# Load order of an mLSTM cell with a mixture-of-depths layer: broadcast maxima with each chunk, layer weights later, output gates half a batch ahead

## The chip, the cores and the metric

The kernel runs on one core of a Trainium2 chip. The metric is the device time of the program in microseconds, the median of several runs. The profile is one execution, recorded by the hardware profiler.

## What is computed

Two blocks stand behind each other. The first is an mLSTM cell over 4 batches of 8 heads, 768 steps, head dimension 40. It is written as a recurrence over steps, with a running maximum m that keeps the exponentials in range:

```python
m_new = np.maximum(f_gate[:, :, t] + m, i_gate[:, :, t])
f_stab = np.exp(f_gate[:, :, t] + m - m_new)
i_stab = np.exp(i_gate[:, :, t] - m_new)
C = f_stab * C + i_stab * np.einsum('bhd,bhe->bhde', vt, kt)
n = f_stab * n + i_stab * kt
h_tilde = np.einsum('bhde,bhe->bhd', C, qt)
denom = np.maximum(np.abs(np.einsum('bhd,bhd->bh', n, qt)), 1.0)
y[:, :, t] = sigmoid(o_gate[:, :, t]) * h_tilde / denom
```

The heads side by side give x (4, 768, 320). The second block scores each token (x times w_gate), takes the 128 best of each batch, puts them through relu(xe @ w1) @ w2 (320 to 1024 to 320), and writes x + sigmoid(score) times that; all other tokens pass through unchanged.

## The kernel before, in words

The 768 steps of a batch are cut into 6 chunks of 128, so that 24 chunks run one after the other, batch by batch, with a state C that goes from chunk to chunk. Ahead of them, a preamble on 32 partitions (batch times head) computes the running maxima of all chunks from the two gate inputs (L138 to L155). Each chunk's maxima `Mg` go to DRAM (`M_d`, L150), since every chunk later wants them broadcast over 128 partitions (`Mb`, L173).

One chunk (`mlstm_chunk`) is this. `Mb` is masked on GpSimd (POOL, affine_select, L174), and eight exponentials on ScalarE (ACT, L178) make the weights `W`. k and q are transposed on TensorE (PE, L185, `pt`) and copied out by ScalarE (`qkT`, L186). `pS` (L195) is the product of k and q, VectorE (DVE) multiplies it with `W` (`P`, L197), `pI` (L204) is what the state gives, `pC` (L218) the state's update, `pH` (L233) the result of the chunk. VectorE adds and scales (`num`, `den`, `rec`), GpSimd multiplies the gate in (`sor`, L245), VectorE writes `x` (L246) and the score `sc` (L249), and GpSimd issues two stores of the chunk, to `x_d` and to `out` (L252). The weights `W`, the maxima `Mb` and most other work tiles have 3 buffers.

After a batch's last chunk, `depths` ranks the tokens (`ge`, `pcol`, `rank`, `sel`), gathers the chosen rows (`xe`), transposes them (`pX`), runs both layers (`ph` L318, `py` L324, copied by ScalarE as `hT`, L320) and scatters `ye` into `out` (L327), behind which the stores of x to `out` wait. Its instructions stand between those of the next batch's first chunks. A scheduler at build time sets the order on each engine; each engine then works in that order.

Loads are issued on SyncE's queue (SPq): k, q and v of a chunk two chunks ahead into 4 rotating buffers (`qk`, `v`, L98, L99), the output gates `so` of a whole batch when it begins (L334, six loads, then one sigmoid over all, L335), and `Mb` of a chunk when the chunk itself is written. The layer weights (`w1`, `w2`, 2.5 MB) and `wg` are loaded by GpSimd's queue after the first batch's gates (L162 to L167). ScalarE needs another function table for the sigmoid than for the exponentials, so each change between them is an ACT_TABLE_LOAD.

Below, chunk 0 to chunk 5 are those of a batch, batch 0 to batch 3.

## Time and profile before

| what | value |
|---|---|
| median of 3 runs | 277.78 us (277.69 to 279.12) |
| profiled execution, its own time | 275.82 us |
| its span, first to last instruction | 274.1 us |
| PE busy | 196.6 us (72%) |
| DVE busy | 153.0 us (56%) |
| ACT busy | 115.8 us (42%) |
| POOL busy | 108.5 us (40%) |
| DMA | 41.08 MB in 107086 packets, mean 150 GB/s |

No engine is busy throughout, so the shares alone name no bound. A profile here is read by stages: what each stage waits for last. The profiled execution took 1.7 us more than its span, and 0.7% less than the median.

### The profile page before, as it was taken

What the parts mean: (1) busy time and instruction counts of PE and PEld (TensorE: products, weight loads), DVE (VectorE), ACT (ScalarE), POOL (GpSimd) and SP (SyncE); (2) the same over time, 40 slices, a digit from 0 to 9 for tenths busy, and PEclk for the clock granted to TensorE, in tenths of its full rate; (3) what the DMA queues carried; (4) which work ended last, traced back from release to release, by engine and by line L of the source; (5) the groups of instructions that cost most, each with busy time, mean ns of one, the idle gap of its engine ahead of it and who ended that gap; (6) DMA issues with size and microseconds to landing.
All of it is one profiled execution on the core that took longest, in us unless ns stands there. A gap on an engine that the chain in (4) does not pass through costs nothing.

```text
span 274.1 us, 6273 instructions
## 1 busy us (share of the span) xinstructions
PE 196.6 (72%) x2402; PEld 164.5 (60%) x2402; DVE 153.0 (56%) x443; ACT 115.8 (42%) x285; POOL 108.5 (40%) x155
## 2 busy tenths in 40 slices
PE   0463089987837999878798997777699998612980
PEld 0442068975626888766677976656488786501860
DVE  5800026597966407878768523897877088873100
ACT  2531486337287653636654181553543325100000
POOL 9900155167264203565454314545463055221001
PEclk9995555599995599999799999797869999965696
DMA  8799997599998633999999709597725041210000
GB/s 119 86 347 183 209 220 196 105 244 188 230 254 241 114 80 82 220 225 246 199 229 190 170 0 215 163 195 223 198 65 134 26 144 57 86 60 24 2 0 24
DMA packets 107086, 41.08 MB, mean 150 GB/s; under 512 B 101328, under 2 KB 101520, under 8 KB 107056
## 3 DMA queue, kind: packets, MB, share of 16 engines
q1 hardware_dynamic: 103680, 28.71, 54.3%
q0 software_dynamic: 3376, 11.96, 13.1%
q8 instruction: 19, 0.31, 0.6%
q14 instruction: 11, 0.09, 0.1%
HBM read 32.05 MB, written 8.62 MB: 148 GB/s over the span
## 4 chain that ended last, share of the span: by engine, by line
PE 31%; DVE 24%; issue 15%; DMA 12%; POOL 7%; SPq 6%; ACT 3%; POOLq 1%; DVEq 0%; ACTq 0%
PE ph L318 6%; PE pS L195 6%; DMA Mb<-M_d 6%; PE pH L233 5%; PE py L324 5%; DVE P L197 4%; DVE C L226 3%; POOL sor L245 3%; PE pI L204 3%; DVE ge L270 3%; SPq L98 2%; PE pt L185 2%; DVE x L246 2%; DVE C L228 2%; SPq L334 2%
## 5 line engine op out<-in xcount | busy, mean ns | idle before, releaser
L178 ACT ACTIVATE W<-Mb,cols 128x128 f32<-128x128 f32 x192 | 59.9, 391 | 34.5 <-POOL Mb L174 19.5
L233 PE MATMUL pH<-v,P 128*64 128x64 f32 x768 | 35.8, 249 | 19.0 <-DVE num L207 11.2
L186 ACT COPY qkT<-pt 128x512 f32<-128x512 f32 x48 | 26.9, 582 | 51.8 <-PE pt L185 51.3
L233 PEld LDWEIGHTS pH<-v,P 128*64 128x64 f32 x768 | 30.3, 157 | 26.7 <-DVE num L207 13.3
L185 PE MATMUL pt<-ident,qk 128*128 128x128 f32 x192 | 35.4, 318 | 15.1 <-ACT so L335 8.4
L195 PE MATMUL pS<-qkT 64*128 64x128 f32 x384 | 39.3, 324 | 1.7 <-ACT qkT L186 1.6
L174 POOL TENSOR_SCALAR_AFFINE_SELECT Mb<-Mb 128x1024 f32<-128x1024 f32 x24 | 26.7, 1116 | 31.3 <-DMA Mb<-M_d 31.3
L185 PEld LDWEIGHTS pt<-ident,qk 128*128 128x128 f32 x192 | 23.8, 158 | 19.6 <-ACT so L335 8.8
L195 PEld LDWEIGHTS pS<-qkT 64*128 64x128 f32 x384 | 31.4, 216 | 6.6 <-ACT qkT L186 3.2
L245 POOL TENSOR_TENSOR sor<-so,rec 128x320 f32<-128x320 f32 x24 | 17.4, 726 | 43.2 <-DVE rec L243 38.0
L197 DVE TENSOR_TENSOR P<-pS,W 128x512 f32<-128x512 f32 x48 | 31.9, 681 | 4.3 <-PE pS L195 3.6
L204 PE MATMUL pI<-C,qkT 128*64 128x128 f32 x320 | 25.9, 301 | 0.7 <-DVE C L228 0.7
L318 PE MATMUL ph<-xeT,w 128*128 128x128 f32 x192 | 25.3, 298 | 0.6 <-DVE g L303 0.6
L318 PEld LDWEIGHTS ph<-xeT,w 128*128 128x128 f32 x192 | 24.6, 212 | 1.6 <-DVE g L303 1.0
L246 DVE TENSOR_TENSOR x<-num,sor 128x320 f32<-128x320 f32 x20 | 12.1, 604 | 19.5 <-POOL sor L245 19.5
L212 POOL TENSOR_TENSOR wv<-v,cols 128x328 f32<-128x328 f32 x20 | 15.1, 755 | 19.1 <-PE pC L218 10.9
L204 PEld LDWEIGHTS pI<-C,qkT 128*64 128x64 f32 x320 | 19.9, 149 | 4.0 <-issue 1.1
L252 POOL DMA_DIRECT2D x_d<-x x24 | 14.0, 582 | 19.2 <-DVE x L246 18.6
L326 DVE SCALAR_TENSOR_TENSOR ye<-py,g,xe 128x320 f32<-128x320 f32 x4 | 2.2, 551 | 34.4 <-PE py L324 34.4
L270 DVE SCALAR_TENSOR_TENSOR ge<-sb,sc,earlier 128x512 bf16<-128x512 f32 (+5 forms) x24 | 16.9, 720 | 3.2 <-ACT sb L262 3.2
L226 DVE TENSOR_TENSOR C<-C,Mb 40x164 f32<-40x164 f32 x32 | 18.3, 571 | 0.5
L324 PE MATMUL py<-w,hT 128*128 128x320 f32 x64 | 17.9, 432 | 0.0
(83 smaller groups left out, 233.2 us busy)
## 6 DMA issues: line engine op xcount, KB each, us to landing
Mb<-M_d SPq DMA_DIRECT2D x24, 516.0 KB, 5.1
qk<-in_k_dram SPq DMA_DIRECT2D x24, 160.0 KB, 4.2
qk<-in_q_dram SPq DMA_DIRECT2D x24, 160.0 KB, 4.7
v<-in_v_dram SPq DMA_DIRECT2D x24, 160.0 KB, 4.2
so<-in_o_gate_dram SPq DMA_DIRECT2D x24, 160.0 KB, 4.2
x_d<-x POOLq DMA_DIRECT2D x24, 160.0 KB, 3.4
out_dram<-x POOLq DMA_DIRECT2D x24, 160.0 KB, 4.0
w<-in_moe_w_dram POOLq DMA_DIRECT2D x1, 1280.0 KB, 10.2
```

Of the source, the lines that this page charges most:

```text
L174: nc.gpsimd.affine_select(out=Mb[:, :, 0:L], in_=Mb[:, :, 0:L], compare_op=OP.is_ge, fill=BIG, base=0, pattern=[[0, H], [1, L]], channel_m ...
L178: nc.scalar.activation(out=W[:, h // 2, h % 2, :], in_=Mb[:, h, 0:L], func=AF.Exp, bias=cols[c][:, 0, b * H + h:b * H + h + 1], scale=-1.0)
L185: nc.tensor.transpose(pt[:, p, :], qk[:, j, 2 * p:2 * p + 2, :].rearrange("s a d -> s (a d)"), ident)
L186: nc.scalar.copy(out=qkT[:, j], in_=pt)
L195: nc.tensor.matmul(pS[j][:, p, :], qkT[e, 0, p, :], qkT[e, 1, p, :], start=True, stop=True)
L197: nc.vector.tensor_tensor(out=P[:, :, j, :], in0=pS[j], in1=W[:, :, j, :], op=OP.mult)
L204: nc.tensor.matmul(pI[t, 2 * p:2 * p + 2, :].rearrange("t a d -> t (a d)"), qkT[:, 1, p, t], C[:, p].rearrange("e a d -> e (a d)"), start= ...
L226: nc.vector.tensor_tensor(out=Cj, in0=Cj, op=OP.mult, in1=decay[e, :, j, L:L + 1].to_broadcast([D, NP, D1]))
L233: nc.tensor.matmul(pH[t, h, :], P[:, h // 2, h % 2, t], v1[:, h, :], start=True, stop=True)
L245: nc.gpsimd.tensor_tensor(out=sor, in0=so[:, c], in1=rec.unsqueeze(2).to_broadcast([128, H, D]), op=OP.mult)
L318: nc.tensor.matmul(ph[:, f, :], w1[:, j, (f0 + f) * 128:(f0 + f + 1) * 128], xeT[:, j, :], start=(j == 0), stop=(j == NDC - 1))
L324: nc.tensor.matmul(py, hT[:, f, :], w2[:, f, :], start=(f == 0), stop=(f == NFC - 1))
```

## The change

The load of `Mb` moves from the chunk itself into `load_chunk`, so that it is issued two chunks ahead, with 4 buffers in place of 3. The stores of `M_d` go from SyncE's queue to ScalarE's. The layer weights are issued when the second chunk is reached (`n == 1`), with `wg` alone left in front. The gates of batch 0 are loaded in two parts, chunks 0 and 1 with their k, q and v, the others after, with a sigmoid for each part. The gates of each later batch are loaded, and put through the sigmoid, in the middle of the batch before (`c == NT // 2`). The memsets of the k, q and v buffers write the padding alone.

```diff
--- before.py
+++ after.py
@@ -88,8 +88,8 @@
     qk_t = [const.tile([128, 2, H, DP], FP, name=f"qk{n}") for n in range(NB)]
     v_t = [const.tile([128, H, DP], FP, name=f"v{n}") for n in range(NB)]
     for n in range(NB):
-        nc.gpsimd.memset(qk_t[n], 0.0)
-        nc.gpsimd.memset(v_t[n], 1.0)
+        nc.gpsimd.memset(qk_t[n][:, :, :, D:DP], 0.0)
+        nc.gpsimd.memset(v_t[n][:, :, D:DP], 1.0)
 
     def load_chunk(b, c):
         n = (b * NT + c) % NB
@@ -97,7 +97,9 @@
         for j, src in enumerate((k, q)):
             nc.sync.dma_start(out=qk_t[n][:, j, :, 0:D], in_=src[b, :, t, :].rearrange("h p d -> p h d"))
         nc.sync.dma_start(out=v_t[n][:, :, 0:D], in_=v[b, :, t, :].rearrange("h p d -> p h d"))
-        return qk_t[n], v_t[n]
+        Mb = work.tile([128, H, L + 1], FP, name="Mb", bufs=NB)
+        nc.sync.dma_start(out=Mb, in_=_bcast(M_d[c][b * H:(b + 1) * H, :], 128))
+        return qk_t[n], v_t[n], Mb
 
     ident = const.tile([128, 128], FP, name="ident")
     make_identity(nc, ident)
@@ -147,7 +149,7 @@
         nc.scalar.activation(out=wk[:, c, :], in_=a[:, c, :], func=AF.Exp, bias=nM[:, c:c + 1], scale=1.0)
         nc.vector.tensor_copy(out=Mg[:, c, L:L + 1], in_=r[:, c, L - 1:L])
         M_d.append(dram.tile([BH, L + 1], FP, name=f"M_d{c}"))
-        nc.sync.dma_start(out=M_d[c], in_=Mg[:, c, :])
+        nc.scalar.dma_start(out=M_d[c], in_=Mg[:, c, :])
         pc = ps_t.tile([128, 3, BH], FP, name="pc", tag="t")
         for j, row in enumerate((a, wk, r)):
             nc.tensor.transpose(pc[:, j, :], row[:, c, :], ident[0:BH, 0:BH])
@@ -158,19 +160,18 @@
     w1 = const.tile([128, NDC, F_], FP, name="w1")
     w2 = const.tile([128, NFC, DM], FP, name="w2")
 
+    nc.gpsimd.dma_start(out=wg, in_=_bcast(moe_w_gate, 128))
+
     def load_weights():
-        nc.gpsimd.dma_start(out=wg, in_=_bcast(moe_w_gate, 128))
         if HW[-1][1] < 128:
             nc.gpsimd.memset(w1[:, NDC - 1, :], 0.0)
         for j, (d0, w) in enumerate(HW):
             nc.gpsimd.dma_start(out=w1[0:w, j, :], in_=moe_w1[d0:d0 + w, :])
         nc.gpsimd.dma_start(out=w2, in_=moe_w2.rearrange("(f p) d -> p f d", p=128))
 
-    def mlstm_chunk(b, c, qk, v1, C, so, x, sc):
+    def mlstm_chunk(b, c, qk, v1, Mb, C, so, x, sc):
         hs = slice(b * H, (b + 1) * H)
         k_n, q_n = qk[:, 0], qk[:, 1]
-        Mb = work.tile([128, H, L + 1], FP, name="Mb")
-        nc.sync.dma_start(out=Mb, in_=_bcast(M_d[c][hs, :], 128))
         nc.gpsimd.affine_select(out=Mb[:, :, 0:L], in_=Mb[:, :, 0:L], compare_op=OP.is_ge, fill=BIG, base=0,
                                 pattern=[[0, H], [1, L]], channel_multiplier=-1)
         W = work.tile([128, NP, 2, L], FP, name="W")
@@ -328,31 +329,47 @@
                                          out_offset=bass.IndirectOffsetOnAxis(ap=idx[:, 1:2], axis=0),
                                          in_=ye, in_offset=None, bounds_check=B * S - 1, oob_is_err=False)
 
+    def load_gates(b, so, c):
+        nc.sync.dma_start(out=so[:, c], in_=o_gate[b, :, c * L:(c + 1) * L, :].rearrange("h p d -> p h d"))
+
     def open_batch(b):
         so = ob.tile([128, NT, H, D], FP, name="so")
-        for c in range(NT):
-            nc.sync.dma_start(out=so[:, c], in_=o_gate[b, :, c * L:(c + 1) * L, :].rearrange("h p d -> p h d"))
-        nc.scalar.activation(out=so, in_=so, func=AF.Sigmoid)
         C = ob.tile([128, NP, 2, DP], FP, name="C")
         nc.gpsimd.memset(C, 0.0)
         x = xp.tile([128, NT, DM], FP, name="x")
         sc = xp.tile([128, NT], FP, name="sc")
         return C, so, x, sc
 
+    def sigmoid(so, c0, c1):
+        nc.scalar.activation(out=so[:, c0:c1], in_=so[:, c0:c1], func=AF.Sigmoid)
+
+
 
     steps = [(b, c) for b in range(B) for c in range(NT)]
-    loaded = {}
+    loaded, state = {}, {0: open_batch(0)}
+    EARLY = 2
     for n, (b, c) in enumerate(steps):
         for step in steps[n:n + AHEAD + 1]:
             if step not in loaded:
                 loaded[step] = load_chunk(*step)
-        if c == 0:
-            state = open_batch(b)
+                if step[0] == 0 and step[1] < EARLY:
+                    load_gates(0, state[0][1], step[1])
+                    if step[1] == EARLY - 1:
+                        sigmoid(state[0][1], 0, EARLY)
         if n == 0:
+            for g in range(EARLY, NT):
+                load_gates(0, state[0][1], g)
+            sigmoid(state[0][1], EARLY, NT)
+        if n == 1:
             load_weights()
-        mlstm_chunk(b, c, *loaded[b, c], *state)
+        if c == NT // 2 and b + 1 < B:
+            state[b + 1] = open_batch(b + 1)
+            for g in range(NT):
+                load_gates(b + 1, state[b + 1][1], g)
+            sigmoid(state[b + 1][1], 0, NT)
+        mlstm_chunk(b, c, *loaded[b, c], *state[b])
         if c == NT - 1:
-            depths(b, *state[2:])
+            depths(b, *state[b][2:])
 
 
 # ---- launch: one core; inputs and outputs as the reference has them ----
```

In the program as built, the start changes as follows. First SyncE's queue before, from the second chunk's k and q on (buffer numbers: qk_94 and v_98 are chunk 0, qk_95 chunk 1, qk_96 chunk 2, M_d_156 the maxima of chunk 0).

```order
L98 DMA qk_95<-in_q_dram 128x8x40
L150 DMA M_d_156<-Mg 32x129
...
L150 DMA M_d_236<-Mg 32x129
L99 DMA v_99<-in_v_dram 128x8x40
L98 DMA qk_96<-in_k_dram 128x8x40
L98 DMA qk_96<-in_q_dram 128x8x40
L99 DMA v_100<-in_v_dram 128x8x40
L334 DMA so<-in_o_gate_dram 128x8x40 x6
L173 DMA Mb<-M_d_156 128x1032
```

SyncE's queue in the changed kernel, from chunk 0's gate on:

```order
L333 DMA so<-in_o_gate_dram 128x8x40
L98 DMA qk_95<-in_k_dram 128x8x40
L98 DMA qk_95<-in_q_dram 128x8x40
L99 DMA v_99<-in_v_dram 128x8x40
L333 DMA so<-in_o_gate_dram 128x8x40
L101 DMA Mb<-M_d_156 128x1032
L101 DMA Mb<-M_d_172 128x1032
L98 DMA qk_96<-in_k_dram 128x8x40
L98 DMA qk_96<-in_q_dram 128x8x40
L99 DMA v_100<-in_v_dram 128x8x40
L101 DMA Mb<-M_d_188 128x1032
L333 DMA so<-in_o_gate_dram 128x8x40 x4
```

The maxima of chunk 0 now stand behind 8 loads in place of 15, and the last gate of batch 0 stands behind the maxima of three chunks. ScalarE in the changed kernel, in the same place (so 128x640 are two chunks' gates, 128x1280 the other four):

```order
L344 ACT_TABLE_LOAD
L344 ACTIVATE so<-so 128x640
L187 COPY qkT<-pt 128x512 x2
L179 ACT_TABLE_LOAD
L179 ACTIVATE W<-Mb,cols_162 128x128 x8
L187 COPY qkT<-pt 128x512 x2
L179 ACTIVATE W<-Mb,cols_178 128x128 x2
L344 ACT_TABLE_LOAD
L344 ACTIVATE so<-so 128x1280
L179 ACT_TABLE_LOAD
L179 ACTIVATE W<-Mb,cols_178 128x128 x6
```

Before, one sigmoid stood ahead of all exponentials; now the second one stands between the second and the third of chunk 1's eight. On the whole, ScalarE has 11 table loads in place of 9.

The second place is TensorE around the layers of batch 0 (pX, ph, py), between the first chunks of batch 1, which are pH with v_100 (chunk 0), v_101 (chunk 1) and v_98 (chunk 2). Before:

```order
L308 MATMUL pX<-ident,xe_130 128x128 x3
L233 MATMUL pH<-v_100,P 64x64 x7
L195 MATMUL pS<-qkT 128x128 x2
L318 MATMUL ph<-xeT,w_245 128x128 x24
L324 MATMUL py<-w_246,hT 128x320 x8
L195 MATMUL pS<-qkT 128x128 x6
L204 MATMUL pI<-C,qkT 64x128 x8
L218 MATMUL pC<-wv,qk_97 64x41 x8
L185 MATMUL pt<-ident,qk_94 128x128 x4
L233 MATMUL pH<-v_101,P 64x64 x16
```

The changed kernel:

```order
L219 MATMUL pC<-wv,qk_97 64x41 x8
L234 MATMUL pH<-v_101,P 64x64 x16
L196 MATMUL pS<-qkT 128x128
L309 MATMUL pX<-ident,xe_130 128x128 x3
L196 MATMUL pS<-qkT 128x128 x3
L205 MATMUL pI<-C,qkT 64x128 x3
L319 MATMUL ph<-xeT,w_245 128x128 x24
L325 MATMUL py<-w_246,hT 128x320 x8
L205 MATMUL pI<-C,qkT 64x128 x5
L219 MATMUL pC<-wv,qk_94 64x41 x8
L186 MATMUL pt<-ident,qk_95 128x128 x3
L234 MATMUL pH<-v_98,P 64x64 x16
```

Before, one chunk of batch 1 stood ahead of the layers; now two do, and the third is begun. At the two later batch ends, two chunks stand ahead of the layers in both kernels.

The third place is GpSimd behind the scatter of batch 1. Before:

```order
L327 DMA out_dram<-ye,idx 3072x320
L252 DMA out_dram<-x 128x320 x2
L245 TENSOR_TENSOR sor<-so,rec 128x320
L252 DMA x_d_136<-x 128x320
```

The changed kernel:

```order
L328 DMA out_dram<-ye,idx 3072x320
L213 TENSOR_TENSOR wv<-v_98,cols_226 128x328
L246 TENSOR_TENSOR sor<-so,rec 128x320
L253 DMA out_dram<-x 128x320 x2
```

The stores to out that wait for the scatter now stand behind the product sor, not ahead of it.

## Rows read from the trace of the kernel before

**Rows 1.** The chain that ended last, shares of the span by engine.

```profile
PE 31%; DVE 24%; issue 15%; DMA 12%; POOL 7%; SPq 6%; ACT 3%; POOLq 1%; DVEq 0%; ACTq 0%
```

**Rows 2.** Timeline, SyncE's queue: start us, us, instruction, count.

```profile
8.60 3.07 SPq L150 DMA_DIRECT2D M_d<-Mg  x6
...
12.83 5.96 SPq L98 DMA_DIRECT2D qk<-in_q_dram  x1
...
21.94 6.29 SPq L334 DMA_DIRECT2D so<-in_o_gate_dram  x6
28.27 0.84 SPq L173 DMA_DIRECT2D Mb<-M_d  x1
```

**Rows 3.** Timeline, ScalarE: start us, us, then idle time before and what ended it.

```profile
31.36 1.28 ACT L335 ACT_TABLE_LOAD   x1 [4.61 <-DMA so<-in_o_gate_dram]
32.65 1.80 ACT L335 ACTIVATE so<-so 128x1920 f32<-128x1920 f32 x1
...
35.77 2.45 ACT L178 ACTIVATE W<-Mb,cols 128x128 f32<-128x128 f32 x8
39.53 2.45 ACT L178 ACTIVATE W<-Mb,cols 128x128 f32<-128x128 f32 x8 [1.32 <-POOL Mb L174]
```

**Rows 4.** Timeline, VectorE: x of chunks 2 and 5 of batch 0.

```profile
62.91 1.01 DVE L246 TENSOR_TENSOR x<-num,sor 128x320 f32<-128x320 f32 x1 [0.52 <-POOL sor L245]
...
79.24 0.49 DVE L246 TENSOR_TENSOR x<-num,sor 128x320 f32<-128x320 f32 x1 [1.15 <-POOL sor L245]
```

**Rows 5.** Windows, one stretch: us, busy us (instructions) by engine, clock, DMA share, GB/s.

```profile
38.70:54.10 15.40, 15.40 (x152) 13.52 (x152) 7.66 (x19) 8.41 (x26) 5.58 (x7) 0.51 0.72 158
```

**Rows 6.** Windows, bounds at x of chunks 5 and 2; columns as above.

```profile
79.30:117.30 38.00, 32.84 (x378) 27.45 (x378) 20.12 (x52) 21.99 (x55) 13.82 (x17) 0.82 0.71 156
117.30:138.50 21.20, 16.18 (x247) 13.72 (x245) 16.51 (x49) 11.65 (x34) 12.53 (x17) 0.92 0.98 220
138.50:171.40 32.90, 29.16 (x362) 24.43 (x362) 17.66 (x52) 15.00 (x36) 11.73 (x15) 1.00 0.77 160
171.40:193.30 21.90, 16.27 (x229) 13.60 (x229) 18.12 (x48) 11.06 (x29) 11.02 (x16) 0.84 0.78 190
193.30:225.00 31.70, 29.12 (x334) 24.51 (x336) 20.50 (x52) 12.88 (x36) 12.28 (x16) 0.89 0.40 105
225.00:243.30 18.30, 11.79 (x223) 10.12 (x219) 15.07 (x47) 4.59 (x12) 6.61 (x10) 0.95 0.22 79
243.30:274.10 30.80, 14.47 (x95) 11.95 (x95) 6.11 (x18) 1.77 (x4) 3.21 (x4) 0.67 0.07 22
```

**Rows 7.** The chain in order of time: start us, us, what. Waits for Mb.

```profile
55.89 5.07 DMA Mb<-M_d
...
124.56 4.42 DMA Mb<-M_d
...
137.06 5.66 DMA Mb<-M_d
```

**Rows 8.** DMA queues: packets, MB, share of 16 engines over the span.

```profile
q1 hardware_dynamic: 103680, 28.71, 54.3%
```

**Rows 9.** DMA queues in the stretch from 12 to 23 us alone.

```profile
q0 software_dynamic: 658, 2.66, 75.5%
```

**Rows 10.** DMA issues: count, KB each, median us to landing.

```profile
Mb<-M_d SPq DMA_DIRECT2D x24, 516.0 KB, 5.1
...
M_d<-Mg SPq DMA_DIRECT2D x6, 16.1 KB, 3.9
```

**Rows 11.** Timeline, GpSimd: the first mask, and behind batch 1's scatter.

```profile
33.21 1.08 POOL L174 TENSOR_SCALAR_AFFINE_SELECT Mb<-Mb 128x1024 f32<-128x1024 f32 x1 [19.66 <-DMA Mb<-M_d]
...
169.49 1.13 POOL L252 DMA_DIRECT2D out_dram<-x  x2 [3.74 <-DMA out_dram<-ye,idx]
170.63 0.73 POOL L245 TENSOR_TENSOR sor<-so,rec 128x320 f32<-128x320 f32 x1
```

**Rows 12.** Groups by line, ScalarE's copies: busy us, mean ns, idle before.

```profile
L186 ACT COPY qkT<-pt 128x512 f32<-128x512 f32 x48 | 26.9, 582 | 51.8 <-PE pt L185 51.3 <-PE pI L204 0.6
```

## The prediction

> **What bounds the kernel now.** I read the chain of what ended last first. TensorE has 31% of it, VectorE 24%, and 18% are transfers and SyncE's queue [rows 1]: no engine is the bound, the order in which things arrive is. So I cut the span at the moments when x of chunk 5 and of chunk 2 is written, and price each stage.
>
> The start comes first. SyncE's queue issues five loads, waits until 8.60 us for the maxima to be computed, stores them, and then issues the rest one after the other, with Mb of chunk 0 as the last of them at 28.27 us [rows 2]. ScalarE waits for the batch's last gate until 31.36, loads a table, runs the sigmoid, loads the table back, and starts chunk 0's weights at 35.77 and chunk 1's at 39.53 [rows 3]. Chunk 2 has its x at 62.91 and chunk 5 at 79.24 [rows 4]. In this stretch TensorE's clock is at its low level: from 38.7 to 54.1 us, 15.4 us long, TensorE is busy all the time at a granted clock of 0.51 [rows 5], about 1.2 of 2.4 GHz.
>
> The later stages are in one table [rows 6]. From chunk 5 to the next batch's chunk 2, with the ranking and the layers between, it takes 38.0, 32.9 and 31.7 us; chunk 2 to chunk 5 takes 21.2, 21.9 and, in the last batch, where nothing is left to load ahead, 18.3 us, or 6.1 a chunk. The tail of 30.8 us after the last chunk is not touched by the change. On the chain there are three waits for Mb, of 5.07, 4.42 and 5.66 us [rows 7].
>
> **The start, step by step.** Six gate loads were issued in 6.29 us with the queue full [rows 2], so a load of 160 KB costs 1.05 us. The SyncE transfers took 54.3% of the 274.1 us span, 148.8 us [rows 8]; less 96 loads at 1.05, that leaves 48 us for 24 Mb, 2.0 us each. The weights took 75.5% of an 11 us stretch, 8.3 us [rows 9].
>
> Mb of chunk 0 now stands behind 8 loads. Its maxima, stored from ScalarE's queue at about 9 us (the row of before has 8.60), land 3.9 us later; Mb takes 5.1 more [rows 10] and its mask 1.08 [rows 11], so it is ready at 19. ScalarE issues the six stores in its own order (3.07 us on SyncE's queue [rows 2]), then runs the short sigmoid, a third of 1.80, between two table loads of 1.28 [rows 3], and two copies of 0.58 [rows 12]: 9 + 3.1 + 4.3, or 16.4. So the mask decides, and chunk 0's weights start at about 19.5, 16 us earlier than before.
>
> That lead is mostly lost at once. ScalarE works in order, and after two of chunk 1's eight exponentials stands the second sigmoid, which waits for the last gate of batch 0. Queued behind it are chunk 1's other exponentials and chunk 2's; VectorE's P and TensorE's pH wait for those. Ahead of that gate the DMA engines move 15 loads (15.8 us), three Mb (6.0), the weights (8.3) and small things (1): 31 us. They begin at about 2.2 us, stand idle for about 1 us while SyncE waits for the stored maxima, and so bring the gate at about 34.5 us, 3 us later than now. Table, sigmoid of four chunks (two thirds of 1.80) and table take 3.8, six exponentials 1.8: chunk 1's weights are complete at 40.1 us. Now they are complete at 39.53 + 2.45 = 41.98, so on this step the change gains under 2 us.
>
> From there chunk 0 is out of the way, and no chunk waits for its Mb, which lands two chunks ahead. Were VectorE's 6.1 us a chunk the pace, chunk 1's x would stand at 46.2 and chunk 2's at 52.3. But TensorE has been idle in the meantime, and in the run of before it then needed the 15.4 us of [rows 5] at the low clock for two chunks' products. At that rate chunk 2's x comes at 40.1 + 15.4 + 3 = 58.5, the 3 being half a chunk's pace for what VectorE does last. I take the middle, 55. With the last batch's 18.3 us for three chunks, chunk 5 is at 73.3 in place of 79.24: a gain of 6 us. Its bounds: 52.3 + 18.3 = 70.6, a gain of 8.6; and 58.5 + 21.9 = 80.4, a loss of 1.2.
>
> **The later stages.** At the first batch end the order puts two of batch 1's chunks ahead of the layers where one stood, as at the two later ends in both kernels. I price it by those: 38.0 becomes 32.9, a gain of 5.1; bounds 0 and 6.3 [rows 6].
>
> Between chunk 2 and chunk 5, batches 1 and 2 need 2.9 and 3.6 us more than the last, which has no loads left. The waits of [rows 7] are longer than that, but other chunks' work lies beside them. I take half, 3.2 us; bounds 0 and 6.5.
>
> Behind batch 1's scatter, GpSimd waits 3.74 us for the scatter to land before it issues two stores, and only then forms sor, for which VectorE's x waits [rows 11]. The new order puts sor first. What is late next is VectorE's own rec, so I take 2.5; bounds 0 and 3.74.
>
> Costs. ScalarE has two table loads more; one is in the 3.8 us above. The other stands in batch 2, where the gates of batch 3 now stand ahead of the layers' g and hT, for which py waits. I take 1 us; bounds 0 and 4.4, a whole table, sigmoid and table (1.28 + 1.80 + 1.28 [rows 3]). The smaller memsets and the earlier clearing of C lie on GpSimd while it waits 19.66 us for the first Mb [rows 11]: nothing; without that cover, under a microsecond.
>
> The rows show the table load at 31.36 followed by the sigmoid at 32.65, with nothing between: 1.28 us is the whole price [rows 3]. The Trainium skill (ScalarE: Activation LUTs, What ACT_TABLE_LOAD costs) adds a drain of about 1.38 us to each switch, and its section on table sets says to batch calls by set, which speaks against cutting the sigmoid in two. By that price the two more loads cost 5.3 us in place of 2.6, and the forecast would be some 2.7 us higher; the trace doesn't show the drain.
>
> **Sum.** 6 + 5.1 + 3.2 + 2.5 - 1 = 15.8 us off the profiled execution's own 275.82 gives 260.0. The median of the runs lies 0.7% above that execution (277.78), so I predict 262 us. All bounds at their best make 25 us, 253 in the runs; all at their worst cost 5.6, 283.
>
> **Rivals.**
> - *The start gives nothing.* The second sigmoid waits longer than I think, or the low clock lasts until chunk 2 is done. For it: during the weights one load of 160 KB took 5.96 us to issue [rows 2], so gates that travel with the weights may be held up. The Trainium skill (DMA: Bandwidth & Descriptors, Queues, rings and completion order) has each DMA engine alternate between its queues packet by packet, by which the weights behind two chunks slow the four gates just as they slowed k and q. Against it: the DMA time is the same and is in my 34.5. Then 15.8 - 6 = 9.8 remain: 268 us.
> - *The later stages give nothing.* The transfers are as many as before, and in batch 1 the DMA share is 0.98 between chunk 2 and chunk 5 [rows 6]; loads that start earlier may only collide with others. Against it: at the batch ends it is 0.71 and 0.77, and there is room. Only 6 - 1 remains, 273 us.
> - *Both*, so that what is moved was hidden anyway: about 278 us.
> - *Slower.* The sigmoid at the head of ScalarE's order holds up all of chunk 1. It decides once it comes 15.8 us later than at 34.5, past 50 us. If four of the loads ahead of the last gate take 5.96 us each in place of 1.05, that is 19.6 us more: 262 + 19.6 = 282. Against it: the weights are only 8.3 us of DMA time, and cannot hold up more than that for long.
>
> **Chances.** My forecast 0.60, its own range 256 to 267; the start gives nothing 0.20; the later stages give nothing 0.10; both 0.05; slower 0.05. 0.5% is about what a measurement of this kernel can tell from no change, so the first three cases count as faster, less some hundredths for values at their upper ends: faster 0.88, same 0.06, slower 0.06. The range goes from 253, all bounds at their best, to 272; it leaves out the two last rivals and half of the one before.
>
> **What would show it.** In the profile after: the first W at about 20 us in place of 35.77; chunk 1's W cut in two, with a table load at about 34.5 that waits for a gate; x of chunk 5 at about 73; no wait for Mb on the chain after the first; the first batch end at 33 us; no sor behind the wait for batch 1's scatter. I am wrong if the table load in chunk 1 comes past 40 us, if TensorE's clock stays low past 60, or if the batch ends take 38 us as before.

## The result, and the profile after

The changed kernel takes 264.83 us (median of 4 runs, 262.5 to 265.88), the kernel before, on the same chip, 277.82 us (277.69 to 279.12): a ratio of 0.951, 95% interval 0.944 to 0.958. Ratios here leave out executions in a slower state, medians are over all of them, so a ratio below can differ by up to 1.5% from that of the two medians beside it. The forecast was 262 us, its range 253 to 272. The execution whose rows follow is the longest of the four, 265.88 us with a span of 264.2.

The same windows as in [rows 6] come first, bounds at x of batch 0's chunk 5 and then alternately at x of chunk 2 and of chunk 5: us, busy us (instructions) of PE, PEld, DVE, ACT and POOL, granted clock of TensorE, DMA share, GB/s.

```profile
0.00:73.70 73.70, 45.58 (x570) 38.00 (x571) 38.41 (x130) 45.03 (x103) 35.43 (x62) 0.86 1.05 220
73.70:110.40 36.70, 32.08 (x363) 26.95 (x361) 19.17 (x51) 17.11 (x44) 15.38 (x19) 0.91 0.80 176
110.40:134.00 23.60, 18.51 (x231) 15.77 (x232) 18.70 (x48) 12.53 (x32) 12.68 (x17) 0.71 0.90 197
134.00:163.60 29.60, 27.64 (x340) 22.95 (x340) 18.55 (x51) 16.58 (x37) 10.28 (x13) 1.00 0.68 145
163.60:186.70 23.10, 17.96 (x267) 15.71 (x261) 19.76 (x50) 11.52 (x32) 13.16 (x19) 0.85 1.00 228
186.70:215.40 28.70, 28.33 (x323) 23.91 (x323) 16.60 (x52) 11.49 (x33) 9.24 (x12) 0.94 0.32 77
215.40:233.30 17.90, 12.14 (x227) 10.41 (x225) 14.72 (x46) 2.24 (x4) 6.60 (x11) 0.95 0.21 76
233.30:264.20 30.90, 14.41 (x95) 11.89 (x95) 6.17 (x18) 1.77 (x4) 3.23 (x5) 0.67 0.07 22
```

Against [rows 4, 6] the start gave 5.5 us (79.2 to 73.7) and the three batch ends 1.3, 3.3 and 3.0; the stretches from chunk 2 to chunk 5 cost 2.4 and 1.2 more, and the last batch gave 0.4. Together that is the 9.9 us by which the span is shorter.

The start keeps near the times of the steps. ScalarE's timeline answers to [rows 3]: start us, us, instruction, count, idle time before and what ended it.

```profile
18.75 1.28 ACT L179 ACT_TABLE_LOAD   x1 [1.41 <-DMA Mb<-M_d]
20.04 2.44 ACT L179 ACTIVATE W<-Mb,cols 128x128 f32<-128x128 f32 x8
...
23.34 0.69 ACT L179 ACTIVATE W<-Mb,cols 128x128 f32<-128x128 f32 x2
35.58 1.28 ACT L344 ACT_TABLE_LOAD   x1 [11.55 <-DMA so<-in_o_gate_dram]
36.87 1.27 ACT L344 ACTIVATE so<-so 128x1280 f32<-128x1280 f32 x1
38.15 1.28 ACT L179 ACT_TABLE_LOAD   x1
39.44 4.20 ACT L179 ACTIVATE W<-Mb,cols 128x128 f32<-128x128 f32 x14
```

Chunk 0's weights start at 20.04 in place of 35.77. Then ScalarE idles for 11.55 us at the second sigmoid, with chunk 1's other six exponentials queued behind. SyncE's queue shows what the last gate was behind: the issue of four gates took 11.74 us while the layer weights moved, which GpSimd had issued from 12.3 to 21.8 us.

```profile
20.57 11.74 SPq L333 DMA_DIRECT2D so<-in_o_gate_dram  x4
```

TensorE's granted clock is 0.50 from 42 to 45 us, 0.62 from 45 to 48 and 1.00 from 48 to 51; before, it was 0.51 up to 54.1 [rows 5]. VectorE writes x of chunks 2 and 5 of batch 0 here, to be compared with [rows 4].

```profile
53.82 0.49 DVE L247 TENSOR_TENSOR x<-num,sor 128x320 f32<-128x320 f32 x1 [0.84 <-POOL sor L246]
...
73.73 0.49 DVE L247 TENSOR_TENSOR x<-num,sor 128x320 f32<-128x320 f32 x1 [1.49 <-POOL sor L246]
```

Last, GpSimd's timeline behind the scatter of batch 0 and of batch 1, which answers to [rows 11]. Behind batch 1's, sor now stands ahead of the stores that wait 2.68 us; behind batch 0's it still comes after them.

```profile
108.48 1.15 POOL L253 DMA_DIRECT2D out_dram<-x  x2 [2.23 <-DMA out_dram<-ye,idx]
109.65 0.73 POOL L246 TENSOR_TENSOR sor<-so,rec 128x320 f32<-128x320 f32 x1
```

```profile
162.89 0.72 POOL L246 TENSOR_TENSOR sor<-so,rec 128x320 f32<-128x320 f32 x1 [0.56 <-DVE rec L244]
166.29 1.16 POOL L253 DMA_DIRECT2D out_dram<-x  x2 [2.68 <-DMA out_dram<-ye,idx]
```

### The profile page after: what moved, and what is told of

It is laid out like the page before. It is cut to its first block, busy times and chain, and to the rows that moved or that the text cites. A ratio compares the mean times of both kernels' runs of the same rounds, so it can differ in the third digit from the quotient of the medians.

```text
span 264.2 us, 6254 instructions
## 1 busy us (share of the span) xinstructions
PE 196.6 (74%) x2402; PEld 165.6 (63%) x2402; DVE 152.1 (58%) x443; ACT 118.3 (45%) x288; POOL 106.0 (40%) x155
## 4 chain that ended last, share of the span: by engine, by line
PE 27%; DVE 19%; issue 16%; DMA 15%; SPq 9%; POOL 9%; ACT 2%; POOLq 1%; DVEq 0%
PE pH L234 5%; PE pS L196 5%; PE ph L319 5%; SPq L333 4%; DVE P L198 4%; DMA xe<-x_d,idx 4%; POOL sor L246 3%; PE py L325 3%; DMA Mb<-M_d 3%; PE pI L205 3%; POOL Mb L175 3%; SPq L99 2%; DVE ge L271 2%; DMA out_dram<-ye,idx 2%; DVE C L227 2%
## 5 line engine op out<-in xcount | busy, mean ns | idle before, releaser
L234 PE MATMUL pH<-v,P 128*64 128x64 f32 x768 | 34.9, 249 | 32.6 <-DVE P L198 20.5
L196 PE MATMUL pS<-qkT 64*128 64x128 f32 x384 | 41.6, 325 | 0.8 <-ACT qkT L187 0.7
L175 POOL TENSOR_SCALAR_AFFINE_SELECT Mb<-Mb 128x1024 f32<-128x1024 f32 x24 | 26.6, 1109 | 30.7 <-DMA Mb<-M_d 25.2
L196 PEld LDWEIGHTS pS<-qkT 64*128 64x128 f32 x384 | 32.9, 218 | 6.7 <-ACT qkT L187 2.5
L186 PE MATMUL pt<-ident,qk 128*128 128x128 f32 x192 | 34.3, 308 | 0.9 <-ACT qkT L187 0.5
L319 PE MATMUL ph<-xeT,w 128*128 128x128 f32 x192 | 26.6, 308 | 0.7 <-DVE g L304 0.7
L319 PEld LDWEIGHTS ph<-xeT,w 128*128 128x128 f32 x192 | 25.9, 222 | 1.6 <-DVE g L304 1.1
L186 PEld LDWEIGHTS pt<-ident,qk 128*128 128x128 f32 x192 | 22.7, 152 | 4.4 <-ACT qkT L187 0.9
L271 DVE SCALAR_TENSOR_TENSOR ge<-sb,sc,earlier 128x512 bf16<-128x512 f32 (+5 forms) x24 | 18.9, 804 | 3.9 <-ACT sb L263 3.9
L247 DVE TENSOR_TENSOR x<-num,sor 128x320 f32<-128x320 f32 x20 | 9.8, 491 | 19.0 <-POOL sor L246 19.0
L227 DVE TENSOR_TENSOR C<-C,Mb 40x164 f32<-40x164 f32 x32 | 17.0, 533 | 0.5
```

The source lines that it names most:

```text
L175: nc.gpsimd.affine_select(out=Mb[:, :, 0:L], in_=Mb[:, :, 0:L], compare_op=OP.is_ge, fill=BIG, base=0, pattern=[[0, H], [1, L]], channel_m ...
L186: nc.tensor.transpose(pt[:, p, :], qk[:, j, 2 * p:2 * p + 2, :].rearrange("s a d -> s (a d)"), ident)
L196: nc.tensor.matmul(pS[j][:, p, :], qkT[e, 0, p, :], qkT[e, 1, p, :], start=True, stop=True)
L234: nc.tensor.matmul(pH[t, h, :], P[:, h // 2, h % 2, t], v1[:, h, :], start=True, stop=True)
L271: nc.vector.scalar_tensor_tensor(out=ge[:, u, 0:n], in0=sb.rearrange("p t l -> p (t l)")[:, 0:n], scalar=sc[:, u:u + 1], in1=earlier[:, NT ...
L319: nc.tensor.matmul(ph[:, f, :], w1[:, j, (f0 + f) * 128:(f0 + f + 1) * 128], xeT[:, j, :], start=(j == 0), stop=(j == NDC - 1))
```

## The experiments

All of them in one table, so that the stages stand side by side. The ratio is to the kernel before on the same chip, with its interval; the stages are those of the windows above (an end runs from x of chunk 5 to x of the next batch's chunk 2), from one profiled execution of each, in us, with the granted clock of the batch ends in brackets. The kernel before has 79.2 | 38.0, 32.9, 31.7 | 21.2, 21.9 there [rows 6].

| kernel | ratio | start | first end | second end | third end | chunk 2 to 5, batches 1 and 2 |
|---|---|---|---|---|---|---|
| changed kernel | 0.951 [0.944, 0.958] | 73.7 | 36.7 (0.91) | 29.6 (1.00) | 28.7 (0.94) | 23.6, 23.1 |
| after_again | 0.972 [0.961, 0.982] | 73.7 | 35.6 (0.86) | 32.8 (0.84) | 26.8 (1.00) | 21.5, 21.1 |
| sig_late | 0.953 [0.945, 0.962] | 73.1 | 33.4 (0.95) | 28.8 (1.00) | 27.1 (1.00) | 21.6, 22.7 |
| sig_late_b | 0.947 [0.939, 0.955] | 73.9 | 32.9 (1.00) | 29.5 (1.00) | 27.0 (1.00) | 21.3, 22.1 |
| nb5 | 0.961 [0.953, 0.969] | 74.4 | 37.5 (0.86) | 31.1 (0.95) | 29.4 (0.93) | 20.5, 22.8 |
| mb_late | 1.008 [1.002, 1.013] | 79.3 | 38.3 (0.78) | 35.1 (0.95) | 35.4 (0.81) | 19.5, 21.4 |
| mb_only | 1.015 [1.009, 1.022] | 79.5 | 35.5 (0.90) | 40.2 (0.83) | 30.4 (0.94) | 20.0, 21.8 |
| w_first | 0.973 [0.963, 0.982] | 74.3 | 38.3 (0.91) | 34.5 (0.90) | 28.7 (0.94) | 21.8, 23.1 |
| gates_at_batch | 0.982 [0.972, 0.991] | 75.5 | 37.1 (0.91) | 31.2 (1.00) | 30.0 (0.94) | 21.4, 21.3 |
| md_sync | 1.030 [1.022, 1.038] | 76.1 | 33.1 (0.95) | 37.1 (0.90) | 38.1 (0.82) | 24.9, 22.1 |
| md_pb | 0.986 [0.977, 0.995] | 76.8 | 35.4 (1.00) | 37.2 (0.91) | 34.5 (1.00) | 21.0, 18.6 |
| sig_wx | 0.978 [0.969, 0.988] | 72.2 | 41.0 (0.71) | 35.0 (0.80) | 34.7 (0.80) | 21.6, 22.3 |
| w_gates_late | 0.929 [0.919, 0.939] | 70.5 | 32.6 (0.90) | 29.1 (0.94) | 28.7 (0.94) | 22.0, 21.5 |

**after_again: the changed kernel unaltered, on another chip.** No edit.

> The changed kernel once more, unaltered, to see how far its stages differ from one execution to the next. If the stages' lengths are set by order and waits, each stage agrees with the first profile within 1 us and the time is 264.8 within 1.5. If TensorE's granted clock, which fell at different moments, sets some of them, then the two long stages between chunk 2 and chunk 5 (23.6 and 23.1 us) and the first batch end (36.7 us, with the first layer at 7.8 us) differ by 2 us or more, with the clock.

It took 267.03 us there (263.0 to 270.01), and the two intervals of this one kernel, 0.944 to 0.958 and 0.961 to 0.982, do not meet: a difference of under 2% between kernels on two chips says nothing. The start is the same to 0.1 us; the second end took 32.8 us in place of 29.6, with the same instructions in the same order. These are its first and second end (columns as in the windows above).

```profile
73.70:109.30 35.60, 33.47 (x364) 27.49 (x363) 17.57 (x51) 17.15 (x44) 15.32 (x18) 0.86 0.85 185
...
130.80:163.60 32.80, 31.47 (x342) 26.32 (x344) 18.12 (x52) 15.98 (x36) 10.40 (x14) 0.84 0.62 137
```

TensorE was busy for 31.47 us of the second end at a clock of 0.84, and for 27.64 us at 1.00 in the profile of the changed kernel: it is the bound there, and the 3 us go with its clock. The two stretches from chunk 2 to chunk 5 differ by 2 us, the shorter ones at the higher clock. The first end does not follow it, 35.6 us at 0.86 against 36.7 at 0.91: there TensorE stood idle for 2.1 us in place of 4.6. A later stage of one execution is known to about 3 us and no better.

**mb_late: Mb loaded in the chunk again, all else as changed.**

```diff
-        Mb = work.tile([128, H, L + 1], FP, name="Mb", bufs=NB)
-        nc.sync.dma_start(out=Mb, in_=_bcast(M_d[c][b * H:(b + 1) * H, :], 128))
-        return qk_t[n], v_t[n], Mb
+        return qk_t[n], v_t[n]
...
-    def mlstm_chunk(b, c, qk, v1, Mb, C, so, x, sc):
+    def mlstm_chunk(b, c, qk, v1, C, so, x, sc):
...
+        Mb = work.tile([128, H, L + 1], FP, name="Mb")
+        nc.sync.dma_start(out=Mb, in_=_bcast(M_d[c][hs, :], 128))
```

> The load of Mb stands in the chunk itself again, with 3 buffers; all other parts of the change stay. Theory: the early Mb at the start is worth the most, since here it stands behind the last gate of batch 0 again; the first exponentials start at about 33 us in place of 20, x of chunk 5 at about 79, and the kernel takes 270 to 273 us. Rival: as the later stages were not shortened by Mb being there, and as chunk 1 waits for the gate anyway, Mb is worth little: the time is within 2 us of 264.8.

278.94 us against 276.72: the whole gain is gone, more than either side expected, at the start (79.3) and at the batch ends. TensorE's order at the ends is nearly that of the changed kernel, with two of the next batch's chunks ahead of the layers, and yet they take 38.3, 35.1 and 35.4. GpSimd's order is not the same: sor stands behind the stores that wait for the scatter at all three ends, in the changed kernel at the first alone. The third end shows the rest. First mb_late, cut into the stretch up to the next chunk's pH, the next 15 us, and the rest; then the same place of the changed kernel.

```profile
188.80:195.70 6.90, 3.98 (x50) 3.02 (x47) 5.56 (x17) 3.41 (x10) 4.34 (x5) 1.00 0.94 244
195.70:210.60 14.90, 14.90 (x152) 12.70 (x154) 9.35 (x28) 4.76 (x14) 4.64 (x6) 0.56 0.41 103
210.60:229.00 18.40, 18.40 (x207) 15.80 (x205) 7.88 (x23) 4.91 (x13) 6.15 (x8) 0.99 0.24 72
```

```profile
182.00:186.80 4.80, 3.78 (x49) 3.03 (x47) 4.72 (x16) 3.72 (x11) 2.50 (x3) 1.00 0.92 209
186.80:200.00 13.20, 12.95 (x168) 10.76 (x168) 9.21 (x28) 6.69 (x20) 4.25 (x6) 0.90 0.39 92
```

In mb_late TensorE stood idle for 2.9 of 6.9 us, and then worked without a pause for 14.9 us at a granted clock of 0.56, most of it at the lower of the two levels (1.2 GHz). In the changed kernel it had 1.0 us of idle time there, and 0.90 behind it. What TensorE waited for in mb_late is on ScalarE and GpSimd, one row of each:

```profile
192.88 0.99 ACT L179 ACTIVATE W<-Mb,cols 128x128 f32<-128x128 f32 x3 [2.66 <-POOL Mb L175]
```

```profile
191.75 1.09 POOL L175 TENSOR_SCALAR_AFFINE_SELECT Mb<-Mb 128x1024 f32<-128x1024 f32 x1 [0.43 <-DMA Mb<-M_d]
192.81 0.72 POOL L246 TENSOR_TENSOR sor<-so,rec 128x320 f32<-128x320 f32 x1
```

The mask of a late Mb stands in GpSimd's order ahead of sor, so that it holds up both W and x. Not all of this is the load: GpSimd waited 0.43 us for Mb, after 1.66 us in which the product ahead of it (wv) had waited for TensorE. So what delays W at a batch's last chunk costs itself and, as far as these rows go, a second time through the clock at which TensorE then does the stage in which it is the bound. ye comes 29.8 us after chunk 5's x, in the changed kernel 25.2; the other 2.1 us of the longer stage lie behind ye.

**mb_only: the kernel before, with Mb loaded in `load_chunk` and nothing else changed.** The diff is the reverse of the one above, with 4 buffers.

> The kernel before with one part of the change alone: Mb is loaded with its chunk's k, q and v, with 4 buffers. Theory: this part brings most of the gain, since taking it away from the changed kernel took the whole gain away (278.9 us); no wait for Mb stalls TensorE between chunks, its clock stays up, and the batch ends, in which TensorE is busy almost all the time, get shorter. The three batch ends fall to 28 to 34 us each and the kernel takes 266 to 270 us. Rival: the parts need each other; alone it leaves one sigmoid ahead of the last exponentials of chunk 0, at the start nothing is gained, and the kernel takes 274 to 278 us.

278.3 us against 274.77. The early load of Mb is needed for the gain and gives none alone: the start stays at 79.5, since one sigmoid over all six gates still stands ahead of chunk 0's last exponentials.

**w_first and gates_at_batch: two parts of the change undone.** The weights issued at chunk 0 (`if n == 1:` taken out ahead of `load_weights()`); the gates of batches 1 to 3 loaded at their own chunk 0.

> The changed kernel with the layer weights issued ahead of chunk 0, as before the change. In its order the second sigmoid comes to stand behind the first exponential of chunk 0, so that chunk 0 waits for the last gate as well. Theory: chunk 0 is lost as a lead, x of chunk 5 of batch 0 comes at 78 to 80 us in place of 73.7, the later stages are as in the changed kernel, 269 to 271 us. Rival: the transfers' total sets the start, whatever comes first: x of chunk 5 within 1 us of 73.7 and the kernel at 263 to 267 us.

269.03 us against 274.77. Chunk 0's x comes at 43.4 in place of 28.0, and chunk 5's at 74.3 all the same: the lead of chunk 0 is worth under 1 us to the start. The ratio of 0.973 cannot be told from that of after_again.

> The changed kernel with the gates of batches 1 to 3 loaded when their batch begins, as before the change. Theory: the sigmoid's 4.4 us lie beside the ranking and the layers, in which TensorE is the bound; the place of the gates is worth under 2 us: 264 to 268 us. Rival: the gates half a batch ahead are what shortened the batch ends; they go back to 33 to 38 us and the kernel takes 270 us or more.

269.78 us against 274.77: up to 2 us more on the start and on each end. With the spread of after_again its stages say no more.

**nb5: one more buffer for each of qk, v and Mb** (`NB = 5`, and one buffer for hT to make room).

> Five buffers for k, q, v and Mb in place of four (and one for hT in place of two, to make room). Theory: between chunk 2 and chunk 5 batches 1 and 2 are long (23.6 and 23.1 us) because SyncE's queue stands still while the layers run, as the next buffers are not free, and then has to load in a burst. With one more buffer these stages fall to 19 to 21 us each and the kernel takes 258 to 260 us. Rival: the volume of transfers or the granted clock (0.71 and 0.85) sets these stages; they keep their length within 1 us and the time stays within 1.5 us of 264.8.

264.65 us; its interval and that of the unaltered kernel on that chip overlap. Chunk 2 to chunk 5 took 20.5 and 22.8 us, where the two profiles of the unaltered kernel have 23.6 and 21.5, 23.1 and 21.1, and the ends stayed: that one more buffer shortens a stage is not shown.

**sig_late: the second sigmoid of batch 0 written behind chunk 1.**

```diff
         if n == 0:
             for g in range(EARLY, NT):
                 load_gates(0, state[0][1], g)
-            sigmoid(state[0][1], EARLY, NT)
...
         mlstm_chunk(b, c, *loaded[b, c], *state[b])
+        if n == EARLY - 1:
+            sigmoid(state[0][1], EARLY, NT)
```

> The second sigmoid of batch 0 is written after chunk 1 in place of before chunk 0, so that all eight exponentials of chunk 1 stand ahead of it. Theory: at the start the wait of ScalarE for the last gate, 11.6 us in the middle of chunk 1, is what counts. Then x of chunk 1 is written at about 34 us in place of 47.9, x of chunk 5 at about 68 in place of 73.7, and the kernel takes about 259 us. Rival: the transfers behind that gate, and the low clock after the wait, set the pace; chunk 1 comes early, chunk 2 waits instead, x of chunk 5 stays at 73 to 74 and the time within 1.5 us of 264.8.

Chunk 1's x comes at 41.9 in place of 47.9, then chunk 2 (54.0) and chunk 5 (73.1) where they were: ScalarE's head-of-line wait of 11.55 us held up chunk 1 alone. What it gave, 261.12 against 267.03 us on one chip, is at the batch ends in the profiles.

**md_sync: the stores of M_d back on SyncE's queue.** Six stores in the first 20 us, and no other edit.

```diff
-        nc.scalar.dma_start(out=M_d[c], in_=Mg[:, c, :])
+        nc.sync.dma_start(out=M_d[c], in_=Mg[:, c, :])
```

> The changed kernel with the stores of M_d on SyncE's queue again. Theory: SyncE waits some 3 us for the maxima with the loads of chunk 1 behind it, the last gate of batch 0 lands 3 us later, and so do chunk 1 and all that follows: x of chunk 5 at about 76.5, the kernel at 267 to 268 us. Rival: the stand-still only moves, since Mb of chunk 0 has to wait for the same stores in either order; nothing changes by more than 1.5 us.

281.69 us against 274.77: slower than the kernel before. The start moved by 2.4 us, as the theory has it. Some 13 to 16 us more were lost behind it (spans of 279.7 against 264.2 and 261.3), where those stores are long done; what differs there in the rows is the built order, which the scheduler made anew, and the clock. Its third end in windows: the last products of chunk 5, TensorE idle, what follows, the wait for the gathered rows, the layers, and the rest up to chunk 2's x.

```profile
186.00:192.30 6.30, 5.55 (x84) 4.31 (x80) 5.58 (x18) 4.00 (x11) 3.65 (x5) 1.00 0.84 250
192.30:195.20 2.90, 0.04 (x1) 0.00 (x0) 2.02 (x4) 0.00 (x0) 2.01 (x3) 1.00 0.56 96
195.20:205.00 9.80, 9.76 (x101) 7.99 (x102) 6.39 (x19) 3.79 (x11) 2.17 (x4) 0.55 0.34 84
205.00:212.20 7.20, 4.02 (x57) 3.44 (x54) 2.17 (x6) 2.83 (x8) 1.94 (x2) 0.90 0.50 121
212.20:225.30 13.10, 13.07 (x81) 11.06 (x83) 3.98 (x13) 1.98 (x5) 2.37 (x3) 0.87 0.11 26
225.30:231.40 6.10, 6.10 (x122) 5.58 (x122) 4.97 (x12) 2.99 (x9) 3.61 (x5) 1.00 0.23 83
```

TensorE's order there has the transpose of chunk 5's scores (pb), which waits for x, ahead of the next chunk's pH; in the changed kernel the rows of TensorE show ten pH and six pS ahead of it. So TensorE idles for 2.9 us, works at 0.55 behind that, idles for 3.2 of 7.2 us until the gather lands, and does the layers at 0.87.

**md_pb: md_sync with work of no use at that place.** Sixteen matmuls go into the tile pb ahead of the last chunk's transpose, which overwrites them.

```diff
             for t in range(n):
+                if t0 + t == NT - 1 and b < B - 1:
+                    for _ in range(16):
+                        nc.tensor.matmul(pb[:, t, :], ident, w2[:, 0, 0:L], start=True, stop=True)
                 nc.tensor.transpose(pb[:, t, :], sc[:, t0 + t:t0 + t + 1].to_broadcast([128, L]), ident)
```

> The kernel with the M_d stores on SyncE's queue (279.7 us, ends 33.1, 37.1 and 38.1 us), with 16 matmuls of no use, 128x128, put into pb ahead of the last chunk's transpose, at which TensorE idled for 2.9 us. Theory: TensorE's idle time there lowers the granted clock, and at the low clock the end, in which TensorE is the bound, gets long. Then with the idle time filled the clock stays at 0.95 or more from chunk 5 to the layers, and the second and third end take 30 to 33 us although 2 to 3 us of work are added; a run about 270 us, a ratio to before of about 0.98. Rival: the built order itself makes them long; they take 37 to 40 us, and the run 280 to 287, a ratio of 1.02 to 1.04.

273.93 us against 277.15, a ratio of 0.986 where md_sync has 1.030 on another chip: with 3.7 us of added work in each of three batches the kernel is some 4% faster. The third end: the added work, and then the stretches up to the layers and with them.

```profile
187.00:191.00 4.00, 3.97 (x36) 3.72 (x34) 2.99 (x10) 2.17 (x7) 2.68 (x5) 1.00 0.78 192
191.00:201.40 10.40, 8.86 (x148) 7.29 (x148) 6.52 (x19) 3.89 (x11) 3.80 (x6) 1.00 0.44 96
201.40:213.40 12.00, 11.70 (x80) 9.70 (x81) 3.50 (x13) 4.70 (x13) 2.25 (x3) 1.00 0.26 73
```

The clock is 1.00 throughout, and ye is there 24.4 us after chunk 5's x, in place of 32.0. That is the theory's side. At the second end it failed: TensorE still waited 1.5 us behind the added work, and the clock was 0.91. The ends as a whole took 35.4, 37.2 and 34.5 us, not the 30 to 33 that it gave: the added work changed the order too, one chunk less stands ahead of the layers, and its work came behind them. And the profile has a mean clock of 0.928, two other executions 0.889 and 0.884, and these took only 0.6 and 0.8 us longer: how much of the gain is the clock is not shown. Windows for the stretch behind the layers, from ye to the x that closes the stage, in the changed kernel, md_sync and md_pb:

```profile
211.90:215.38 3.48, 3.46 (x69) 3.15 (x69) 2.17 (x8) 1.08 (x2) 2.51 (x3) 1.00 0.12 44
```

```profile
225.28:231.40 6.12, 6.12 (x122) 5.59 (x122) 4.99 (x12) 2.99 (x9) 3.61 (x5) 1.00 0.23 83
```

```profile
213.42:223.47 10.05, 9.05 (x173) 8.10 (x173) 7.43 (x19) 3.52 (x10) 5.00 (x7) 1.00 0.28 83
```

It is 3.5, 6.1 and 10.1 us, with TensorE busy for nearly all of it. In the built order of the third end, 16 of the next batch's pI stand ahead of the layers in the changed kernel, 8 in md_sync, and in md_pb 8 with the pH of one chunk in place of two. So a batch end has two parts. Up to ye it is long where TensorE waits and its clock is low; behind ye it is longer where less of chunk 2 is already done and where sor stands behind the stores, which mostly go together here.

**sig_wx: sig_late with the weights held back until chunk 2's x.**

```diff
-        if n == 1:
+        if n == 3:
+            for w in (w1, w2):
+                nc.vector.tensor_copy(out=w[:, 0:2, 0:1], in_=state[0][2][:, 2, 0:2].unsqueeze(2))
             load_weights()
```

> sig_late, with the layer weights made to wait for batch 0's chunk 2 (a tiny copy of its x into w1 and w2 stands ahead of their loads), so that they are issued at about 54 us in place of 12 to 21. Theory: the start is set by the sum of the transfers. Then the four gates, whose issue took 11.7 us beside the weights, take about 5; chunk 1's x comes at about 35 in place of 41.9, chunk 5's at 66 (65 to 69) in place of 73.1, and the run takes about 7 us less than the kernel with the late sigmoid, a ratio to before of about 0.93. Rival A: the weights meet batch 1's gates and loads and give it back; the start as above, but chunk 2 to 5 of batch 1 or the first batch end is some 5 us longer, ratio 0.95. Rival B: the start is paced by the engines, chunk 5 at 71 to 74, ratio 0.95 to 0.96.

One of the four weight loads, 256 KB, does not wait for the copy and was issued at 14.4 us; the others came at 48. The kernel took 275.3 us against 277.15, longer than all three sides expected. Its profile, an execution of 277.07 us, is read for the start alone. The four gates were issued in 4.42 us in place of 11.7, and chunk 2's x came at 44.6 in place of 54.0, as the theory has it; then chunk 3 took until 56.8, and chunk 5 stood at 72.2. GpSimd's timeline shows a wait that no side had named: wv of batch 1's chunk 0 waits 8.49 us for its v, issued at 50.94 while the weights moved, and behind it stands the sor of batch 0's chunk 4.

```profile
61.34 0.74 POOL L213 TENSOR_TENSOR wv<-v,cols 128x328 f32<-128x328 f32 x1 [8.49 <-DMA v<-in_v_dram]
62.04 0.72 POOL L246 TENSOR_TENSOR sor<-so,rec 128x320 f32<-128x320 f32 x1
```

**w_gates_late: sig_late, weights held back until chunk 1's x, later gates at chunk 4.** As above with `n == 2` and chunk 1's x, and `c == NT // 2 + 1` for the gates.

> The kernel with the late sigmoid, with the layer weights made to wait for chunk 1's x of batch 0 (in place of chunk 2's, as in the last try) and the gates of a later batch issued at chunk 4 in place of 3. GpSimd's products for chunks 2 and 3 then stand where they stood, and at the second and third batch end TensorE's order ahead of the layers is that of the kernel with the late sigmoid. Theory: the start is set by what is transferred ahead of chunk 2, and a GpSimd product that waits for the next batch's v, in front of chunk 4's sor, gave the gain back. Then x of chunk 1 stands at about 36, chunk 2 at 46, chunk 5 at 66 to 68 in place of 73.1, the second and third end take 27 to 30 us, and a run is about 6 us shorter than with the late sigmoid alone, a ratio to before of about 0.93. Rival: the sum of all transfers up to chunk 5 sets the start, the weights only change places; chunk 5 at 71 to 74, and the two kernels are equal within 1%.

256.44 us against 276.7, the shortest median of all. Chunk 1 at 36.5 and chunk 2 at 44.9 as the theory has it, chunk 5 at 70.5: between the theory and its rival. The ratio is the theory's 0.93, where sig_late_b has 0.947 on the same chip; the medians are 2.8 us apart, not 6. On its chain up to there stand two transfers of the same sort as in sig_wx. GpSimd waits 1.12 us for the first (wv) and 2.21 for the second (the mask), with sor right behind them:

```profile
47.73 6.67 DMA v<-in_v_dram
...
62.34 6.23 DMA Mb<-M_d
```

**sig_late_b: sig_late once more, on that chip.** No edit.

> The kernel with the late sigmoid unaltered, on the same chip as the run before it. Theory: what it gained over the changed kernel is in the built order and in TensorE's clock at the batch ends, not chance, so the ratio to before is again 0.945 to 0.96, with the second and third end at 27 to 30 us. Rival: the one profile was a lucky one; the ratio is 0.96 to 0.98, as the changed kernel's, and an end of 32 us or more is in the profile.

259.19 us, a ratio of 0.947, and its ends are 32.9, 29.5 and 27.0: what sig_late's profile showed was not chance. How much it gains over the changed kernel is less sure, since that kernel, whose ratios are 0.951 and 0.972, was not run on this chip.

## Why the prediction was right, and where its steps were not

**The start: right.** 73.7 was forecast as 73.3, W at 20.04 as 19.5, the second sigmoid's table load at 35.58 as 34.5, chunk 2's x at 53.8 as 55. The table load and the sigmoid stand back to back, 3.86 us in all (3.8 forecast). The Trainium skill (ScalarE: Activation LUTs, What ACT_TABLE_LOAD costs) adds about 1.38 us of drain to each switch; the rows at 38.15 and 39.44 leave no room for it. One step was right by its sum alone: the issue of the four gates took 11.74 us beside the weights, and 4.39 with the weights out of the way (w_gates_late). The Trainium skill (DMA: Bandwidth & Descriptors, Queues, rings and completion order) has each DMA engine alternate between its queues packet by packet; by that rule the weights slow the gates, and these two numbers agree. And the reason given for the gain, chunk 0's lead and the exponentials, did not hold either: w_first and sig_late move those by 15 and 6 us and leave chunk 5 at 73 to 74. No one part accounts for the 5.5 us: chunk 5 is at 79.3 without the early Mb, 79.5 with it alone, and 76.1 with the stores of M_d back on SyncE's queue. With the weights and the next batch's gates held back it is at 70.5, with the weights alone at 72.2. That it moves with what is transferred ahead of it fits this but is not shown: in gates_at_batch, which holds back the next batch's gates alone, it is at 75.5.

**The first batch end, -5.1 us: the step failed.** It gave 1.3 here and 2.4 in after_again. The prediction said that two chunks ahead of the layers make the end 33 us. Windows of the first end, cut at the layers and at ye, before and after:

```profile
79.24:93.06 13.82, 9.70 (x91) 7.32 (x91) 8.21 (x22) 10.61 (x35) 5.75 (x6) 0.57 0.83 196
93.06:103.85 10.79, 10.79 (x68) 9.24 (x67) 0.99 (x3) 5.10 (x7) 1.34 (x2) 0.92 0.51 93
103.85:117.23 13.38, 12.28 (x223) 10.86 (x223) 10.91 (x26) 6.34 (x14) 6.73 (x9) 1.00 0.75 165
```

```profile
73.73:90.39 16.66, 12.65 (x177) 9.99 (x175) 12.70 (x38) 9.02 (x30) 8.24 (x9) 0.93 0.93 200
90.39:102.56 12.17, 12.17 (x67) 10.63 (x68) 1.18 (x5) 6.41 (x14) 2.42 (x3) 0.81 0.76 162
102.56:110.41 7.85, 7.23 (x123) 6.30 (x123) 5.29 (x10) 1.65 (x3) 4.71 (x6) 1.00 0.58 143
```

The second chunk's work changed sides: 5.5 us less stand behind ye, and 2.8 more ahead of the layers. Against the second end of the kernel before, by which the step priced it (14.25, 9.97 and 8.64 us for the same three parts), the first end now takes 2.4 us more ahead of the layers, where TensorE waited 2.98 us for the gathered rows in place of 0.74, 2.2 more in the layers, at a clock of 0.81 in place of 1.00, and 0.8 less behind ye. So the clock and the wait for the rows are what the step left out. In after_again the parts are 17.13, 10.53 and 7.99 us, with the low clock, 0.70, ahead of the layers. The number of chunks is too coarse: mb_late has two ahead and took 38.3, and at a clock of 1.00 sig_late_b took 32.9 us at the first end and 27.0 at the third, where chunk 2's pI stands ahead as well and sor ahead of the stores.

**Chunk 2 to chunk 5, -3.2 us: wrong.** The two stretches took 46.7 us in place of 43.1, and 42.6 in after_again, so between 3.6 us lost and 0.5 gained. The rival "the later stages give nothing" was right here. The clock may be part of it (0.71 and 0.92 for 23.6 and 21.5 us of the same instructions); w_gates_late still needed 22.0 and 21.5 at a clock of 1.00, with a DMA share of 1.02 and 1.10. That the transfers bound it is argued from this, not shown.

**sor ahead of the stores, -2.5 us: right.** In both kernels ye of batch 1 comes 24.2 us after chunk 5's x, at a clock of 1.00. These are the windows from ye to the x that closes the stage, before and after:

```profile
162.75:171.39 8.64, 6.79 (x115) 5.85 (x115) 4.25 (x11) 2.33 (x4) 3.78 (x5) 1.00 0.88 172
```

```profile
158.17:163.64 5.47, 5.45 (x96) 4.81 (x98) 4.16 (x10) 1.08 (x2) 3.60 (x4) 1.00 0.52 101
```

The difference is 3.2 us, within the bound of 3.74. In after_again the stretch takes 5.8 us. No run changes this place alone, but over all of them the stretch takes 2.8 to 6.0 us where sor stands ahead of the stores and 5.9 to 10.3 where it stands behind.

**The third table load, +1 us: nothing.** The sigmoid of batch 3's gates stands ahead of the exponential for g, which is done at 150.20 us, while ph runs from 148.20 to 153.8 and py follows without a pause.

**No wait for Mb on the chain after the first: wrong.** One of 3.60 us stands at 155.5, and GpSimd still waits 25.2 us for Mb in ten places.

**The third end, -3.0 us, was not forecast.** 2.7 of it lie behind ye (3.5 us in place of 6.2): the built order has 16 of the next batch's pI ahead of the layers in place of 8, chunk 2's with chunk 1's, and sor ahead of the stores.

The sum was 15.8 us; the medians differ by 13.0, the two profiled executions by 9.9. The forecast was right on its start and on sor; its two middle terms, 8.3 us together, lost 2.3 in the first profile and gave 2.9 in the second. That the time came within 3 us of 262 is in part luck: the third end, which was not seen, gave 3.0 and 4.9 us, the third table load cost nothing, and 3 us are between the profiles and the medians. What stays open is how much of md_sync's loss is the order itself and how much the clock that its gaps cost: md_pb changed both.

## What to carry to other kernels

Price a stage in which an engine is the bound at the clock that it will have, and look for what makes TensorE idle just ahead of it: 2.9 us of idle time in place of 1.0 ahead of the third end went with 4.6 us more up to ye in mb_late. Where a scheduler sets the order, any edit makes a new order everywhere; compare the built order stage by stage, and have a second edit with little meaning of its own, as md_sync was, before a gain or loss far from the edit is put down to it. On an engine that works in order, put nothing that waits for a load ahead of the product on the path: here wv or the mask stood ahead of sor in the kernels read, and the fastest has 12.9 us of transfers for them on its chain before chunk 5 of batch 0.

## What the runs showed of the hardware

TensorE's granted clock was low after idle time of its own, and the work that followed took longer: a mean of 0.56 over 14.9 us in mb_late after 2.9 us of idle time, 0.55 over 9.8 us in md_sync after as much. The length of the wait does not set it alone: in sig_late a wait of 2.88 us up to 172.0 was followed by 0.84 over the next 10 us, and in the kernel before one of 1.99 us up to 119.9 by 1.00. The first layer, 48 matmuls in the profile, took 5.62 us at 1.00 and 7.83 us where the clock was low for part of it, in one execution of the changed kernel:

```profile
90.39 7.83 PE L319 MATMUL ph<-xeT,w 128*128 128x128 f32 x48
...
148.20 5.62 PE L319 MATMUL ph<-xeT,w 128*128 128x128 f32 x48
```

With work of no use in it a kernel ran in 273.9 us and without it in 281.7, on two chips whose medians of the kernel before are 277.2 and 274.8; its order differs too.
